# One down product of the last chunk as seven smaller products, with its token sums made earlier

## The chip, the cores and the metric

The kernel runs on one core of a Trainium2 chip. The metric is the device time of one execution in microseconds (us), as the median over runs. The core has TensorE (PE in the profile: matmuls; PEld: its weight loads), VectorE (DVE), ScalarE (ACT), GpSimd (POOL) and SyncE (SP, whose queue issues nearly all DMAs here). Matmuls write PSUM banks; the other data lies in SBUF.

## The reference

Four residual layers over x of 2048 tokens x 1024: linear attention, gated MLP, linear attention, gated MLP. The change touches the gated MLP:

```python
def _B_ref(x, W_gate, W_up, W_down):          # D = 1024, F = 3584
    gate = x @ W_gate                         # einsum bsd,df->bsf
    up = x @ W_up
    gate = gate * (gate > 0)
    h = gate * up
    return h @ W_down                         # einsum bsf,fd->bsd
x = x + _B_ref(_layernorm(x), W_gate, W_up, W_down)
```

## The kernel before, in words

Layers are numbered 0 to 3; the gated MLPs are 1 and 3. Each works on two chunks (c = 0, 1) of 1024 tokens, so (3, 1) is the very last chunk. A chunk has 14 gated units (u), each making two 128-wide pieces of h for all its tokens, and then the down stage (`down`).

All large products use the Strassen-Winograd scheme: a 2x2 block product by seven products, with sums of blocks before and after. In the gated units four banks of token sums (s1 to s4) and four sums of weights are used; the halves of tokens and of F give four blocks of h for each pair of units, kept in seven tiles hT[0..6]. In the down stage the seven products are called "11", "21", "T1", "T2", "22", "T3", "T4"; each is a 14-step accumulation over h, or over a sum of h blocks (e1, e2, third_sum), against a part of W_down or a sum of its parts. W_down's sums were made once, early, and lie in DRAM.

A down product is done in one of two ways:

- `product`: four banks of 128x512, 56 matmuls of 512 columns, weights in two ring entries of 896 KB, bank by bank handed to `done`.
- `deep`: the product is itself cut by the same scheme into seven products (1, 5, 6, 2, 7, 3, 4 in order of issue) of 14 matmuls of 256 columns on three banks x, y, z. Its token sums S1 to S4 are made on VectorE before (`inner`), its weight sums come from DRAM (`self.dd`, made by `make_dd`: load, four sums, seven stores), in four ring entries (`load_deep`; three of 896 KB, one of 448 KB). Between the products stand ScalarE copies (y from x after product 1, m5 from z after product 5) and one VectorE addition (z = y + m5 after product 6, line 1495). Products 7 and 4 accumulate on y, product 3 on z.

`is_deep` says which products of which chunk are deep. In (3, 1) the order is "11", "T2", "T1", "T3", "21", "22", "T4", and T1, 22, T4 and 21 are deep; "11" is a plain `product` on banks X. When a bank of "11" is done, `eleven_done` copies it to a bank of Y (ScalarE, line 1535), onto which T2 then accumulates, and adds it to the residual x (VectorE, line 1430).

The order of the work. TensorE, VectorE, ScalarE, GpSimd and SP each take their own instructions in the order in which the program was scheduled at build time. The scheduler walks the program in traced order: of the instructions of an engine that are ready by its own model, the one traced first goes first. The kernel places background work by ticks: `later.at(n, f)` traces f after n more ticks, one tick for each group of matmuls (four in a gated unit); `behind(self.last_put, ...)` keeps it on its engine behind the last `put` (the VectorE multiplication that writes h). A gated unit has 14 ticks, fewer where some of its products are made ahead (`inner_gi`): 10 in unit 12 of (3, 1), 12 in unit 13. Weights arrive through a ring of depth 5: reaching an entry traces the load of the one five places on. Ring entries, hT, e1, e2, s1 to s4, normalised tokens and `make_dd`'s two tiles share 16 buffers of 8 KB a partition, given out in traced order.

At the start of `down`, VectorE makes third_sum and, for each of seven tiles of h, e2 (line 1384) and e1 (line 1385); all are traced ahead of the first product. T2 uses e2, T1 uses e1.

In layer 1, chunk 1, the units also carry `ln_early` (layer norm statistics of the next layer), sums of the next layer's weights (`load_w`, `sums_w`), sums for later gated units (`make_gi`) and, from unit 6, `make_dd("T4")`. In (3, 1) the residual tiles x[0] to x[7], whose chunk is done, hold data of `inner_gi` (`ready_gi(5, 0, 2, 6)`, `ready_gi(6, ..., 4, 7)`) until unit 11.

Of the kernel before, what the change touches and what calls it, by code (L numbers as in the profile page):

```python
# [8 lines left out]
ALU = mybir.AluOpType  # L9
ACT = mybir.ActivationFunctionType  # L10
F32 = mybir.dt.float32
BF16 = mybir.dt.bfloat16
F16 = mybir.dt.float16
PSUM = bass.MemoryType.PSUM
P = 128
NW = 512
HD = 32
QT = 4
# [52 lines left out]
class _Later:  # L71
# [5 lines left out]
    def at(self, delay, fn):  # L77
        self.n += 1
        self.tasks.append((self.now + delay, self.n, fn))
# [13 lines left out]
class _Net:  # L93
# [903 lines left out]
                        out=t[:, 0:self.U // 2, :].bitcast(src.dtype), in_=src))  # L997

    T_AT = {"T1": 0, "T3": 1, "T4": 2, "T2": 3}
    DEEP = ("T1", "22", "T4", "21")  # L1000

    def is_deep(self, l, c, p):
        return p in {(1, 0): ("T1", "22"), (3, 1): self.DEEP}.get((l, c), self.DEEP[:3])

    def order_d(self, l, c):
        if (l, c) == (3, 1):
# [366 lines left out]
    def down(self, l, c, hT, final):  # L1373


        nc, later, ring, v = self.nc, self.later, self.ring, self.nc.vector
        N, H, NK = NW, NW // 2, self.U // 2
        pairs = [(p, [x[:, b::4, :] for b in range(4)]) for p, x in enumerate(hT)]
        e1, e2 = ([self.slot(f"e{i}_{l}_{c}_{k}", dtype=F16) for k in range(2)] for i in (1, 2))
        part = lambda e, p: e[p // 4][:, (p % 4) * 2:(p % 4) * 2 + 2, :]  # L1380
        with self.tc.issue_after(self.last_put.ins):
            self.third_sum(hT[-1])
            for p, (a, _, g, d) in pairs:
                v.tensor_tensor(out=part(e2, p), in0=d, in1=g, op=ALU.subtract)
                v.tensor_tensor(out=part(e1, p), in0=part(e2, p), in1=a, op=ALU.add)
        raw = lambda b: lambda k: hT[k // 2][:, (k % 2) * 4 + b, :]
        own = lambda e: lambda k: e[k // 8][:, k % 8, :]

        def of_h(b):
            return [([hT[p][:, b::4, :] for p in range(3)] + [hT[3][:, b:b + 1, :]]),  # L1390
                    ([hT[p][:, b::4, :] for p in range(4, 7)] + [hT[3][:, b + 4:b + 5, :]])]

        def of_e(e):
            return [[e[0][:, i:i + 2, :] for i in (0, 2, 4)] + [e[0][:, 6:7, :]],
                    [e[1][:, i:i + 2, :] for i in (0, 2, 4)] + [e[0][:, 7:8, :]]]

        def cut(pieces, j):
            return [x[:, :, j * H:(j + 1) * H] for x in pieces]

        def room(b):  # L1400
            return [cut(x, j) for x in of_h(b) for j in range(2)]

        X = [self.ps.tile([P, N], F32, tag="a", name=f"dx{j}") for j in range(QT)]
        Y = [self.ps3.tile([P, N], F32, tag="b", name=f"dy{j}") for j in range(2)]
        Y += [self.kvp.tile([P, N], F32, tag=f"kv{j}", name=f"dy{2 + j}") for j in range(2)]
        first, second = c * 2 * QT, (c * 2 + 1) * QT
# [30 lines left out]
                self.last_on = v.tensor_tensor(out=xo[:, s, :], in0=xs[:, s, :], in1=src[:, s, :], op=ALU.add)  # L1437
                queue.dma_start(out=self.o_v[:, ts.start + s.start:ts.start + s.stop, cols], in_=xo[:, s, :])

        def sums(ops):  # L1440

            for out, a, b, how in ops:
                for o, x, y in zip(out, a, b):
                    yield lambda o=o, x=x, y=y, how=how: v.tensor_tensor(out=o, in0=x, in1=y, op=how)

        def inner(A, S):
            S1, S2, S4, S3 = S
            (a11, a21), (a12, a22) = ([cut(A[k], j) for j in range(2)] for k in range(2))
            return (a11, a12, a22, S1, S2, S3, S4), list(sums((
                (S1, a21, a22, ALU.add), (S2, S1, a11, ALU.subtract),  # L1450
                (S3, a11, a21, ALU.subtract), (S4, a12, S2, ALU.subtract))))

        def deep(p, parts, put, cut_y=False):

            a11, a12, a22, S1, S2, S3, S4 = parts
            B = {}

            def entry(e):
                ring.free_before((l, c, p, e))
                w = self.deep_view(ring.get((l, c, p, e)))  # L1460
                raw = w if p[0] != "T" else w[:, :, :, :].bitcast(F16)
                made = w[:, :, :, :].bitcast(F16)
                B.update(({1: raw[:, 0], 5: made[:, 1]}, {6: made[:, 0], 2: raw[:, 1]},
                          {7: made[:, 0], 3: raw[:, 1]}, {4: made[:, 0]})[e])

            def mm(m, A, bank, start=False):
                for j in range(2):
                    out = bank[j] if isinstance(bank, list) else bank[:, j * H:(j + 1) * H]
                    for i in range(NK):
                        nc.tensor.matmul(out,  # L1470
                                         lhsT=A[i // 2][:, i % 2, j * P:(j + 1) * P], rhs=B[m][:, i, :],
                                         start=start and i == 0 and j == 0, stop=i == NK - 1,
                                         skip_group_check=True)
                    if m == 4 and cut_y:
                        put(1, 0, [out if i == j else None for i in range(2)], True)

            x, y, z = (self.ps.tile([P, N], F32, tag="a", name=f"d{n}{p}") for n in "xyz")
            m5 = self.temp(name="dm5")
            copy = lambda out, src: nc.scalar.activation(out=out, in_=src, func=ACT.Copy)
            halves = lambda a: [a[:, j * H:(j + 1) * H] for j in range(2)] if cut_y else [a]  # L1480
            ys = [y]
            if cut_y:
                ys = y = [y[:, 0:H], self.kvp.tile([P, N], F32, tag="kv0", name=f"dv{p}")[:, 0:H]]
            entry(0)
            mm(1, a11, x, True)
            for o, i in zip(ys, halves(x)):
                copy(o, i)
            later.tick()
            mm(5, S1, z, True)
            copy(m5, z)  # L1490
            later.tick()
            entry(1)
            mm(6, S2, y)
            for o, i, b in zip(halves(z), ys, halves(m5)):
                v.tensor_tensor(out=o, in0=i, in1=b, op=ALU.add)
            later.tick()
            mm(2, a12, x)
            put(0, 0, x, True)
            early = p != "T1"
            if early:  # L1500
                put(1, 1, m5, False)
            later.tick()
            entry(2)
            mm(7, S3, y)
            put(1, 1, y, early)
            later.tick()
            mm(3, S4, z)
            put(0, 1, z, True)
            if not early:
                put(1, 1, m5, True)  # L1510
            later.tick()
            entry(3)
            mm(4, a22, y)
            if not cut_y:
                put(1, 0, y, True)
            later.tick()

        def put_into(t, n):
            def put(j, h, src, last):
                if isinstance(src, list):  # L1520
                    for i, s in enumerate(src):
                        if s is not None:
                            at = t + 2 * j + i
                            onto(slice(at, at + 1), slice(n * N + h * H, n * N + (h + 1) * H), s, last,
                                 (nc.scalar, nc.sync)[i])
                    return
                onto(slice(t + 2 * j, t + 2 * j + 2), slice(n * N + h * H, n * N + (h + 1) * H), src, last)
            return put

        def put_both(j, h, src, last):  # L1530
            for a in range(2):
# [35 lines left out]
            to(first, 0, X, False)(j)  # L1567

        if self.is_deep(l, c, "21"):
            product("11", raw(0), X, True, eleven_done)  # L1570
            parts, jobs = inner(of_e(e1), room(0))
            spread(jobs, 1, 3)
            product("T2", own(e2), Y, False, to(first, 1, Y, False))
            for p, (_, b, _, _) in pairs:
                later.at(2 + p // 2, lambda b=b, p=p: sub(part(e2, p), b, part(e2, p)))
            deep("T1", parts, put_both)
            parts, jobs = inner(of_h(1), room(0))
            spread(jobs, 1, 3)
            product("T3", raw(2), Y, False, third_done)
            parts2, jobs = inner(of_e(e2), room(2))  # L1580
            spread(jobs, 1, 4)
            deep("21", parts, put_into(first, 0))
            parts, jobs = inner(of_h(3), room(0))
            spread(jobs, 1, 4)
            deep("22", parts2, put_into(first, 1))
            deep("T4", parts, put_into(second, 0), final and c == 1)
            return
# [20 lines left out]
    def plan_inner(self, l, c, u, hT):  # L1608
# [34 lines left out]
        if (l, c) == (3, 1):  # L1643
            if u == 0:
                at(4, lambda: ready(5, 0, 2, 6))
            if u == 1:
                at(4, lambda: ready(6, self.slot("gw", [P, 32 * P], F16), 4, 7))
        for m, us in self.INNER.get((l, c), {}).items():
            if u + 2 in us and (u + 2 - us[0]) % 2 == 0:
                at(10 if u + 2 == us[0] else 1, lambda m=m: self.load_gi(m, u + 2))  # L1650

    def layer_B(self, l, final):
# [6 lines left out]
        for c in range(2):  # L1659
# [3 lines left out]
            for u in range(self.U):  # L1663
# [26 lines left out]
                self.plan_inner(l, c, u, hT)  # L1690
                if u % 2 == 0 and u:
                    self.later.at(7, lambda h=hT[-2]: self.behind(self.last_put, self.third_sum, (h,)))
                if (l, c, u) in ((1, 1, 6), (3, 0, 5)):
                    self.make_dd("T4" if l == 1 else "21", 1)
                if c == 0 and u == 1:
                    for n, turn in enumerate(self.turns):
                        self.later.at(1 + n, turn)
# [75 lines left out]
```

## Time and profile before

| | |
|---|---|
| median of 3 runs | 1439.17 us (1439.04 to 1439.54) |
| span of the profiled execution | 1437.3 us |
| around the span, by the median | 1.9 us |
| PE busy | 1429.1 us (99%), 7706 matmuls |
| DVE busy | 1035.7 us (72%), 1991 instructions |
| ACT busy | 622.2 us (43%), 1137 instructions |
| "11" of the last chunk in the chain | 1354.23 us, for 12.09 us |
| mean DMA rate | 231 GB/s |

One execution was profiled; its own time is given by its span, with what lies around it taken from the median of the runs. Rows of a timeline give the start in us from the span's start, the duration, the engine, the source line, the operation, out<-in with the program's names and the number of instructions merged; in brackets, the idle time of the engine before it and what ended it. "SPq" rows are DMAs as SP's queue issues them. [...] A windows row gives the stretch, its length, and for PE, PEld, DVE, ACT and POOL the busy us and the number of instructions, then the granted TensorE clock, the DMA share and GB/s.

### The profile page before, as it was taken

How to read it: one execution, taken by the hardware profiler on the slowest of the kernel's cores; microseconds unless marked ns; L12 is line 12 of the kernel's file. 1: busy time of each engine (PE TensorE's matmuls, PEld its weight loads, DVE VectorE, ACT ScalarE, POOL GpSimd, SP SyncE). 2: the span in 40 equal slices, each digit the busy share in tenths (PEclk: the TensorE clock that was granted, in tenths of full speed). 3: DMA queues.
4: the chain of work that ended last, by engine and by line, in shares of the span. 5: the costliest groups of instructions: out<-in, count | busy, mean ns of one | idle time of the engine just before them, and what ended most of it. 6: DMA issues, size and time to landing. Idle time of an engine off the chain costs nothing.

```text
span 1437.3 us, 21281 instructions
## 1 busy us (share of the span) xinstructions
PE 1429.1 (99%) x7706; PEld 735.6 (51%) x7706; DVE 1035.7 (72%) x1991; ACT 622.2 (43%) x1137; POOL 309.0 (21%) x220
## 2 busy tenths in 40 slices
PE   9999999999999999999999999999999999999998
PEld 4444444444456444545654444445554565555457
DVE  7978698778685676558778885865766764666785
ACT  7873564233425234332058725733443434444201
POOL 1453860010100010110031577410111011111102
PEclk9999999999999999999999999999999999999999
DMA  9950787999659999866983118998878799775565
GB/s 284 243 162 8 171 208 201 292 317 292 204 190 308 350 355 334 278 216 209 292 281 100 60 22 248 278 281 261 263 226 297 225 305 281 215 203 170 175 238 180
DMA packets 360889, 331.31 MB, mean 231 GB/s; under 512 B 109840, under 2 KB 321296, under 8 KB 359760
## 3 DMA queue, kind: packets, MB, share of 16 engines
q1 hardware_dynamic: 352208, 307.15, 71.7%
q10 hardware_dynamic: 7136, 18.88, 3.5%
q0 software_dynamic: 1440, 3.93, 0.8%
q8 instruction: 60, 0.98, 0.3%
q14 instruction: 45, 0.37, 0.1%
HBM read 243.66 MB, written 61.60 MB: 212 GB/s over the span
## 4 chain that ended last, share of the span: by engine, by line
PE 94%; DVE 4%; ACT 1%; issue 0%; DMA 0%; DVEq 0%; ACTq 0%
PE ps L506 11%; PE yu L1275 9%; PE yg L1275 9%; PE dy L1417 8%; PE xg L1275 7%; PE xu L1275 6%; PE dx L1417 6%; PE i L1128 5%; PE ps L789 4%; PE zu L1275 3%; PE zg L1275 3%; PE my L588 3%; PE dyT L1470 2%; PE mv L588 2%; PE mx L588 2%; PE vu L1275 2%
## 5 line engine op out<-in xcount | busy, mean ns | idle before, releaser
L1275 PEld LDWEIGHTS <-w 128*128 128x128 f16 (+1 forms) x2768 | 270.6, 98 | 295.0 <-issue 3.7
L506 PE MATMUL ps<-w,xnT 128*128 128x512 bf16 x768 | 169.9, 379 | 0.7 <-DVE xnT L356 0.3
L1355 POOL TENSOR_TENSOR h<-m5u,m5g 128x512 f16<-128x512 f32 x28 | 37.1, 1326 | 423.4 <-DVE m5u L1351 253.4
L506 PEld LDWEIGHTS <-xnT 128*128 128x128 bf16 x768 | 74.3, 98 | 90.5 <-issue 1.8
L1275 PE MATMUL xg<-xnT,w 128*128 128x512 f16 x448 | 115.3, 379 | 0.0
L1275 PE MATMUL xu<-xnT,w 128*128 128x512 f16 x448 | 115.0, 379 | 0.0
L1417 PEld LDWEIGHTS <-h 128*128 128x128 f16 x672 | 65.7, 98 | 78.3
L1470 PEld LDWEIGHTS <-h 128*128 128x128 f16 x966 | 94.5, 98 | 12.3
L1355 POOL TENSOR_TENSOR h<-c22u,c22g 128x512 f16<-128x512 f32 x28 | 35.6, 1271 | 289.9 <-DVE c22u L1351 247.6
L1275 PE MATMUL yu<-s,w 128*128 128x512 f16 x376 | 96.5, 379 | 0.5 <-DVE zu L1331 0.5
L1275 PE MATMUL yg<-s,w 128*128 128x512 f16 x376 | 96.8, 379 | 0.0
L449 ACT ACTIVATE e<-e,eps 128x512 f32<-128x512 f32 x128 | 91.0, 720 | 3.2
L736 POOL TENSOR_TENSOR kvc<-pq,kvc 128x1024 f32<-128x1024 bf16 x32 | 78.6, 2455 | 53.1 <-DVE den L741 32.7
L1417 PE MATMUL dx<-w,h 128*128 128x512 bf16 x392 | 85.3, 379 | 0.0
L789 PE MATMUL ps<-T,pqT 128*128 128x512 bf16 x384 | 83.6, 379 | 0.0
L1302 DVE TENSOR_TENSOR h<-yu,r 128x512 f16<-128x512 f32 x56 | 38.6, 690 | 55.8 <-PE yu L1275 55.8
L1299 ACT ACTIVATE r<-yg 128x512 f32<-128x512 f32 x56 | 33.4, 597 | 101.5 <-PE yg L1275 101.5
L527 POOL TENSOR_TENSOR kvc<-kvc,slab 128x512 f32<-128x512 f32 x46 | 57.2, 1248 | 76.0 <-DVE slab L452 72.7
L448 ACT ACTIVATE e<-ps 128x512 f32<-128x512 f32 x92 | 54.2, 589 | 28.6 <-PE ps L506 28.1
L1128 PEld LDWEIGHTS <-x 128*128 128x128 f16 x504 | 49.2, 98 | 33.5 <-issue 1.9
L1299 ACT ACTIVATE r<-zg 128x512 f32<-128x512 f32 x56 | 32.8, 586 | 70.8 <-PE zg L1275 70.8
L748 POOL TENSOR_TENSOR pq<-pq,den 128x1024 bf16<-128x1024 bf16 x32 | 61.2, 1914 | 6.8 <-DVE den L743 6.8
(274 smaller groups left out, 2597.0 us busy)
## 6 DMA issues: line engine op xcount, KB each, us to landing
w<-in_B_W_gate_dram SPq DMA_DIRECT2D x56, 512.0 KB, 6.1
w<-in_B_W_up_dram SPq DMA_DIRECT2D x56, 512.0 KB, 5.4
w<-ddT SPq DMA_DIRECT2D x21, 896.0 KB, 6.3
w<-td SPq DMA_DIRECT2D x18, 896.0 KB, 4.8
x<-away SPq DMA_DIRECT2D x30, 512.0 KB, 7.5
w<-dd SPq DMA_DIRECT2D x15, 896.0 KB, 5.9
w<-in_B_W_down_dram SPq DMA_DIRECT2D x14, 896.0 KB, 6.1
away<-x SPq DMA_DIRECT2D x24, 512.0 KB, 6.8
```

Of the source, the lines that this page charges most:

```text
L449: self.last_exp = nc.scalar.activation(out=e, in_=e, func=ACT.Exp, scale=-1.0, bias=self.eps6[:, 0:1])
L506: nc.tensor.matmul(by_row(ps), lhsT=self.xnT[l, l_q][:, kt, j * P:(j + 1) * P], rhs=w[:, kt, :].rearrange("p (b i d) -> p i b d", i=R, d=H ...
L588: nc.tensor.matmul(banks[j], lhsT=A(i)[:, j * P:(j + 1) * P], rhs=B(i), start=start and i == 0, stop=i == NS - 1, skip_group_check=True)
L736: nc.gpsimd.tensor_tensor(out=prod, in0=pq_of[sc, j], in1=zrow, op=ALU.mult)
L748: nc.gpsimd.tensor_tensor(out=heads(pq), in0=heads(pq), in1=den[:, :].unsqueeze(2).to_broadcast([P, D // HD, HD]), op=ALU.mult)
L789: nc.tensor.matmul(ps, lhsT=pqT[sc][:, g, j * P:(j + 1) * P], rhs=T[g // 4][:, g % 4, n2 * NW:(n2 + 1) * NW], start=(g == 0), stop=(g == G ...
L1128: nc.tensor.matmul(b[:, w, :], lhsT=B[p][:, w, k, :], rhs=A[p][:, k, :], start=start and w == 0 and k == 0, stop=k == 1, skip_group_check= ...
L1275: nc.tensor.matmul(ps, lhsT=W[w][m][:, k, :], rhs=A[m][:, k, :], start=start and k == 0, stop=k == 3, skip_group_check=True)
L1299: self.last_relu = nc.scalar.activation(out=out, in_=ps, func=ACT.Relu)
L1355: nc.gpsimd.tensor_tensor(out=h[:, 3, :], in0=V["u"], in1=V["g"], op=ALU.mult)
L1417: nc.tensor.matmul(banks[j], lhsT=A(k)[:, j * P:(j + 1) * P], rhs=w[:, i, :], start=start and k == 0, stop=k == self.U - 1, skip_group_che ...
L1470: nc.tensor.matmul(out, lhsT=A[i // 2][:, i % 2, j * P:(j + 1) * P], rhs=B[m][:, i, :], start=start and i == 0 and j == 0, stop=i == NK - ...
```

## The change

"11" of (3, 1) becomes deep. `DEEP` gets "11" as a fifth member, so its weight sums are made in DRAM like those of the others: `make_dd("11", 1)` runs in layer 1, chunk 1, from unit 0 on. The ring of (3, 1) holds four entries for "11" in place of two.

The sixteen token sums of "11" (four kinds, four pieces each) are no longer work of the down stage: `first_sums` places twelve at ticks 1 to 6 of unit 12 and four, those that need h of units 12 and 13, at tick 7 of unit 13, into x[0], x[1], x[6] and x[7]. At the head of the down stage all e1 are traced behind all e2. The four banks X are not taken. `put_first` adds each finished block to the residual and copies it, in halves, to the banks of Y by ScalarE. Inside `deep`, for "11", the sum that ends in the second row's second block is first made in m5 (m5 = y + m5 after product 7) and put after product 3.

```diff
-    DEEP = ("T1", "22", "T4", "21")
+    DEEP = ("T1", "22", "T4", "21", "11")
...
+    def first_sums(self, hT, homes):
+        S = []
+        for t in homes:
+            h = self.x[t].bitcast(F16)[:, 0:self.U // 2 * (NW // 2)].rearrange("p (k n) -> p k n", n=NW // 2)
+            S.append([h[:, i:min(i + 2, 7), :] for i in range(0, 7, 2)])
+        self.first_parts, jobs = self.quarters(self.pieces(hT, 0), S)
+        return [jobs[i::4] for i in range(4)]
...
+            e1_of = lambda p, a: v.tensor_tensor(out=part(e1, p), in0=part(e2, p), in1=a, op=ALU.add)
             for p, (a, _, g, d) in pairs:
                 v.tensor_tensor(out=part(e2, p), in0=d, in1=g, op=ALU.subtract)
-                v.tensor_tensor(out=part(e1, p), in0=part(e2, p), in1=a, op=ALU.add)
+                if not self.is_deep(l, c, "11"):
+                    e1_of(p, a)
+            if self.is_deep(l, c, "11"):
+                for p, (a, _, _, _) in pairs:
+                    e1_of(p, a)
...
-            early = p != "T1"
+            early = p not in ("T1", "11")
...
             mm(7, S3, y)
-            put(1, 1, y, early)
+            if p == "11":
+                v.tensor_tensor(out=m5, in0=y, in1=m5, op=ALU.add)
+            else:
+                put(1, 1, y, early)
...
+        def put_first(j, h, src, last):
+            put_into(first, 0)(j, h, src, False)
+            for i in range(2):
+                nc.scalar.activation(out=Y[2 * j + i][:, h * H:(h + 1) * H], in_=src[:, i * H:(i + 1) * H],
+                                     func=ACT.Copy)
...
-            product("11", raw(0), X, True, eleven_done)
+            if self.is_deep(l, c, "11"):
+                deep("11", self.first_parts, put_first)
+            else:
+                product("11", raw(0), X, True, eleven_done)
...
+            if u == self.U - 2:
+                self.first = self.first_sums(hT, (0, 1, 6, 7))
+                for i, n in enumerate((3, 0, 1)):
+                    for k, job in enumerate(self.first[n]):
+                        at(1 + 2 * i + k // 2, lambda job=job: self.behind(self.last_put, lambda j: j(), (job,)))
+            if u == self.U - 1:
+                for job in self.first[2]:
+                    at(7, lambda job=job: self.behind(self.last_put, lambda j: j(), (job,)))
...
-                if (l, c, u) in ((1, 1, 6), (3, 0, 5)):
-                    self.make_dd("T4" if l == 1 else "21", 1)
+                if (l, c, u) in ((1, 1, 0), (1, 1, 6), (3, 0, 5)):
+                    self.make_dd({0: "11", 6: "T4", 5: "21"}[u], 1)
```

The functions `pieces`, `token_half` and `quarters` are the former inner functions `of_h`, `cut`, `sums` and `inner` of `down`, moved out so that `first_sums` can use them; for the other deep products they give the same instructions as before.

More of the change, by code (lines that the diff above doesn't have):

```diff
@@ L999, with pieces, token_half, quarters @@
     T_AT = {"T1": 0, "T3": 1, "T4": 2, "T2": 3}
-    DEEP = ("T1", "22", "T4", "21")
+    DEEP = ("T1", "22", "T4", "21", "11")
     def is_deep(self, l, c, p):
         return p in {(1, 0): ("T1", "22"), (3, 1): self.DEEP}.get((l, c), self.DEEP[:3])
+    def pieces(self, hT, b):
+        return [([hT[p][:, b::4, :] for p in range(3)] + [hT[3][:, b:b + 1, :]]),
+                ([hT[p][:, b::4, :] for p in range(4, 7)] + [hT[3][:, b + 4:b + 5, :]])]
+    def token_half(self, pieces, j):
+        return [x[:, :, j * NW // 2:(j + 1) * NW // 2] for x in pieces]
+    def quarters(self, A, S):
+        v = self.nc.vector
+        S1, S2, S4, S3 = S
+        (a11, a21), (a12, a22) = ([self.token_half(A[k], j) for j in range(2)] for k in range(2))
+        jobs = [lambda o=o, x=x, y=y, how=how: v.tensor_tensor(out=o, in0=x, in1=y, op=how)
+                for out, a, b, how in ((S1, a21, a22, ALU.add), (S2, S1, a11, ALU.subtract),
+                                       (S3, a11, a21, ALU.subtract), (S4, a12, S2, ALU.subtract))
+                for o, x, y in zip(out, a, b)]
+        return (a11, a12, a22, S1, S2, S3, S4), jobs
+    def first_sums(self, hT, homes):
[5 more added lines that the diff above has]
+        return [jobs[i::4] for i in range(4)]
     def order_d(self, l, c):
@@ L1382, in down @@
             self.third_sum(hT[-1])
+            e1_of = lambda p, a: v.tensor_tensor(out=part(e1, p), in0=part(e2, p), in1=a, op=ALU.add)
             for p, (a, _, g, d) in pairs:
                 v.tensor_tensor(out=part(e2, p), in0=d, in1=g, op=ALU.subtract)
-                v.tensor_tensor(out=part(e1, p), in0=part(e2, p), in1=a, op=ALU.add)
+                if not self.is_deep(l, c, "11"):
[3 more added lines that the diff above has]
+                    e1_of(p, a)
         raw = lambda b: lambda k: hT[k // 2][:, (k % 2) * 4 + b, :]
         own = lambda e: lambda k: e[k // 8][:, k % 8, :]
-        def of_h(b):
-            return [([hT[p][:, b::4, :] for p in range(3)] + [hT[3][:, b:b + 1, :]]),
-                    ([hT[p][:, b::4, :] for p in range(4, 7)] + [hT[3][:, b + 4:b + 5, :]])]
+        of_h = lambda b: self.pieces(hT, b)
         def of_e(e):
@@ L1395, in of_e @@
                     [e[1][:, i:i + 2, :] for i in (0, 2, 4)] + [e[0][:, 7:8, :]]]
-        def cut(pieces, j):
-            return [x[:, :, j * H:(j + 1) * H] for x in pieces]
         def room(b):
-            return [cut(x, j) for x in of_h(b) for j in range(2)]
-        X = [self.ps.tile([P, N], F32, tag="a", name=f"dx{j}") for j in range(QT)]
+            return [self.token_half(x, j) for x in of_h(b) for j in range(2)]
+        if not self.is_deep(l, c, "11"):
+            X = [self.ps.tile([P, N], F32, tag="a", name=f"dx{j}") for j in range(QT)]
         Y = [self.ps3.tile([P, N], F32, tag="b", name=f"dy{j}") for j in range(2)]
@@ L1438, in onto @@
                 queue.dma_start(out=self.o_v[:, ts.start + s.start:ts.start + s.stop, cols], in_=xo[:, s, :])
[L1440 to L1451, printed above, removed]
+        inner = self.quarters
         def deep(p, parts, put, cut_y=False):
```

## The prediction

> **What bounds the kernel now.** I read the page first (busy times, then the chain that ended last), then who TensorE (PE) waited for.
>
> ```profile
> span 1437.3 us, 21281 instructions
> PE 1429.1 (99%) x7706; PEld 735.6 (51%) x7706; DVE 1035.7 (72%) x1991; ACT 622.2 (43%) x1137; POOL 309.0 (21%) x220
> PE 94%; DVE 4%; ACT 1%; issue 0%; DMA 0%; DVEq 0%; ACTq 0%
> ```
>
> ```profile
> PE idle L302 <- DVE e L299: 1.4, 1, 1.4
> PE yu L1275 <- DVE zu L1331: 0.5, 1, 0.5
> ```
>
> TensorE is busy for 99% of the span and 94% of the chain; its longest single wait is 1.4 us, at the very start, and none of the others is above 0.5 us. So the time is the matmul stream. A change pays by what it takes from that stream, and loses by every hole it opens in it. Nothing else counts here. The span is 1437.3 us; the median of the runs is 1439.17 us, so 1.9 us lie around the span, and I carry those over unchanged. Then the chain at the place of the change, in order of time:
>
> ```profile
> 1354.23 12.09 PE dx L1417 x56
> 1366.31 12.09 PE dy L1417 x56
> 1378.40 1.53 PE dxT L1470 x14
> ...
> 1401.31 1.53 PE dx L1470 x14
> ```
>
> The columns are start, duration, group. The first row is the product "11" of the last chunk as it is; the second is T2; the last two are one of the seven small products of T1 (f16 weights) and of "21" (bf16 weights, as "11" has).
>
> **The change part by part.**
>
> **1. The matmuls.** 56 of 512 columns (12.09 us) go; 7 groups of 14 of 256 columns come, 7 x 1.53 = 10.71 us. The gain is 12.09 - 10.71 = 1.38 us, 0.10% of the time. It is the only term with a minus sign, and it is smaller than 0.2% (2.9 us), which is about what a measurement of this kernel can tell from no change.
>
> [...]
>
> **2. The sum that now stands between the products.** In the old "11" VectorE (DVE) fed nothing to TensorE until T1. In the new one the fifth product (S3, on the bank y) and the sixth (S4, on z) both need z = y + m5, a VectorE addition, done: the fifth overwrites what it reads, the sixth accumulates on what it writes. What VectorE does at that time:
>
> ```profile
> 1354.33 0.69 DVE L1302 TENSOR_TENSOR h<-yu,r 128x512 f16<-128x512 f32 x1 [1.04 <-PE yu L1275]
> 1354.94 0.68 DVE L1384 TENSOR_TENSOR e<-h 128x1024 f16<-128x1024 f16 x1
> 1355.54 0.68 DVE L1371 TENSOR_TENSOR h<-h 128x1024 f16<-128x1024 f16 x1
> ...
> 1361.56 1.28 DVE L1384 TENSOR_TENSOR e<-h 128x1024 f16<-128x1024 f16 x2
> 1362.77 1.28 DVE L1385 TENSOR_TENSOR e<-e,h 128x1024 f16<-128x1024 f16 x2
> 1363.97 1.27 DVE L1430 TENSOR_TENSOR x<-x,dx 128x512 f32<-128x512 f32 x2
> 1365.17 1.09 DVE L1444 TENSOR_TENSOR h<-e,e 128x512 f16<-128x512 f16 x3
> ...
> 1383.15 0.69 DVE L1495 TENSOR_TENSOR dzT<-dyT,dm 128x512 f32<-128x512 f32 x1
> ```
>
> ```profile
> 1361.88 0.58 ACT L1535 ACTIVATE dy<-dx 128x512 f32<-128x512 f32 x1 [7.82 <-PE dx L1417]
> ```
>
> ```profile
> 1354.06 6.21 PE L1417 MATMUL dx<-w,h 128*128 128x512 bf16 x28
> ```
>
> From 1354.94 to 1363.97 it makes the fifteen sums of the stage's head (third_sum, seven e2, seven e1) without a gap, 0.60 us apart. The change reorders the e1 behind the e2, but all fifteen stay ahead of the new product in the program. That program order decides is seen in the last rows: the first dx bank was ready for its addition once ScalarE's (ACT) copy of 1361.88 ended, at 1362.46, yet the addition ran at 1363.97, after two more e1. So z = y + m5 should run at 1363.97 and end 0.69 us later (the row of 1383.15 is the same operation in T1), at 1364.66. Without a wait the fifth product would start after four, at 1354.06 + 4 x 1.53 = 1360.18 (1354.06 is where the matmuls of "11" begin). The hole is 4.48 us. Nothing can fill it: the sixth product needs the same sum, the seventh comes after the fifth on y, T2 accumulates onto banks that the later products of "11" still have to seed, and T1 is behind weights whose buffers "11" still holds. Bounds: 0, if the sum is issued ahead of the e1; 5.1 us, if the fifteen start one operation later. I take 4.5, from the row itself.
>
> [...]
>
> **3. The rest of the product's tail.** Two ScalarE copies of 128x256 in place of one 128x512 for each block: 2 x 0.37 us (the row below), after an addition of 0.69 us, against a last product of 1.53 us; hidden, 0 (up to 0.3). VectorE's work in the old eleven_done (four additions) stays; z and the sum m5 are two more, 1.4 us, which later work makes up in idle stretches of T2 (the second row ends one of 0.69 us).
>
> ```profile
> 1424.33 0.37 ACT L1479 ACTIVATE dyT<-dxT 128x256 f32<-128x256 f32 x1 [8.57 <-PE dxT L1470]
> ```
>
> ```profile
> 1373.90 0.69 DVE L1430 TENSOR_TENSOR x<-x,dy 128x512 f32<-128x512 f32 x1 [0.69 <-PE dy L1417]
> ```
>
> **4. The weights on SyncE's (SP) queue.** Four ring entries (3 of 896 KB and one of 448) in place of two. The first three rows of loads for the old "11" and T2:
>
> ```profile
> 1343.87 0.34 SPq L996 DMA_DIRECT2D w<-td  x1
> 1354.26 0.34 SPq L996 DMA_DIRECT2D w<-td  x1
> 1354.69 0.38 SPq L1023 DMA_DIRECT2D w<-ddT  x1
> ```
>
> ```profile
> DMA to landing us min/median/max: 6.2/6.2/6.2
> ```
>
> These places in the queue (depth five) now carry entries 2 and 3 of "11" and the first of T2. The last one landed 6.2 us after its issue at 1354.69, at 1360.9; entry 2 is needed at 1360.2 but leaves at 1343.87, entry 3 leaves at 1354.26 for 1363.2, T2 needs its own at 1364.8. 0 us; a hole would have to come from a load 4 us later than these.
>
> **5. Sixteen token sums in units 12 and 13.** By the row of 1365.17 a 128x512 sum costs (1.09 - 0.42) / 2 = 0.33 us of VectorE, a 128x256 one 0.20 (rows below, 1366.77 to 1366.97); 12 x 0.33 + 4 x 0.20 = 4.8 us, 3.4 of them in unit 12.
>
> ```profile
> 1366.77 0.28 DVE L1444 TENSOR_TENSOR h<-e 128x256 f16<-128x256 f16 x1
> 1366.97 0.41 DVE L1444 TENSOR_TENSOR h<-h,e 128x512 f16<-128x512 f16 x1
> ```
>
> ```profile
> 1334.00:1344.00 10.00, 10.00 (x50) 4.69 (x48) 6.71 (x11) 3.41 (x7) 1.27 (x1) 1.00 0.27 92
> 1344.00:1354.00 10.00, 10.00 (x48) 4.49 (x46) 4.80 (x7) 3.42 (x6) 1.27 (x1) 1.00 0.52 185
> ```
>
> ```profile
> 1336.82 0.70 DVE L1331 TENSOR_TENSOR zg<-yg,x 128x512 f32<-128x512 f32 x1
> ```
>
> ```profile
> 1337.63 0.81 PE L1275 MATMUL yg<-s,w 128*128 128x512 f16 x3
> ```
>
> VectorE (fourth figure after the stretch: 6.71 and 4.80 us of 10) has 8.5 us free, so the work fits. But in unit 12 the sums are traced ahead of zg, and TensorE starts yg at 1337.63, 0.11 us after zg ends at 1337.52. Four sums (1.1 us) can come between; TensorE has the second product of u to do meanwhile. 0 to 1.5 us, taken 0.5, nearer the fit.
>
> **6. The weights' sums, made in layer 1, chunk 1.** make_dd("11") is 3 loads (1792 KB), 4 sums and 7 stores (3136 KB) in units 0 to 2.
>
> ```profile
> 490.00:500.00 10.00, 10.00 (x48) 4.45 (x46) 10.00 (x23) 4.29 (x10) 1.27 (x1) 1.00 1.11 337
> 500.00:510.00 10.00, 10.00 (x48) 4.55 (x47) 8.85 (x21) 4.58 (x8) 1.27 (x1) 1.00 1.06 358
> ```
>
> ```profile
> L1051 DVE TENSOR_TENSOR dd<-dd x4: 1079/1080/1083, 295.1 to 1042.4; 128x1792 f16<-128x1792 bf16 x4
> ```
>
> ```profile
> 498.80 0.67 DVE L1331 TENSOR_TENSOR zg<-yg,m5g 128x512 f32<-128x512 f32 x1
> ```
>
> ```profile
> 499.00 0.59 PE L1275 MATMUL vu<-s,w 128*128 128x512 f16 x2
> 499.52 1.02 PE L1275 MATMUL yg<-s,w 128*128 128x512 f16 x4
> ...
> 505.99 1.03 PE L1275 MATMUL xu<-xnT,w 128*128 128x512 f16 x4
> ```
>
> ```profile
> 485.64 1.96 SPq L1172 DMA_DIRECT2D w<-in_B_W_up_dram  x1
> ```
>
> Here VectorE is full (10.00 of 10, then 8.85) and the DMA engines too (shares 1.11 and 1.06), and TensorE starts yg at 499.52, 0.05 us after zg's end. Four sums of 1.08 us, 4.3 us, fall due from the middle of unit 1 on, ahead of such sums; TensorE has covered such lateness with the next unit's first products (vu at 499.00, two of its four matmuls, ahead of this unit's yg). 0 to 2.2 us (half of the 4.3), taken 0.5. The 4.9 MB at 350 GB/s are 14 us of transfers, in front of ring loads on SP's queue and, for the stores, held until VectorE's sums are done. The load issued at 485.64 feeds the matmuls of 505.99, 20 us later: 0, up to 1.
>
> **Sum.** -1.38 + 4.5 + 0.5 + 0.5 = +4.1 us: span 1441.4, time 1443.3 us, 0.29% slower.
>
> **The rivals.**
> *The wait is not there* (ends on the other side, not slower). The scheduler issues z = y + m5 between the e2 and the e1; eight sums end at 1354.94 + 8 x 0.60 = 1359.8, then z to 1360.5, a hole of 0.3 us. It decides at one point: whether z stands ahead of more than half of the e1. For it: the change does move the e1 back. Against: the held-back additions above. -1.38 + 0.3 + 0 to 1.0 = 1438.1 to 1439.1, no change that can be told.
> *The wait costs more than itself.* TensorE's first matmuls of the kernel, out of idleness, ran slow:
>
> ```profile
> 1.35 3.62 PE L302 MATMUL idle<-e 128*128 128x512 bf16 x10 [1.35 <-DVE e L299]
> ```
>
> Ten in 3.62 us, where ten at 216 ns and a drain of 0.16 take 2.3. If a hole of 4.5 us brings that back, 1.3 us come on top: 1444.6. Against it, no row shows a hole of that size. [...]
> *Parts 5 and 6 are the cost, not the wait.* Both at their ends: -1.4 + 0.3 + 1.5 + 2.2 = +2.6, 1441.8. Against it, TensorE showed no waits in those stretches.
>
> **How the numbers follow.** The forecast 0.55, no wait 0.27, wait and clock 0.13, the sums 0.05. Faster by over 0.2% would be below 1436.3; the only gain is 1.4 us, so 0.02. Within 0.2%: no wait, the sums, and the low end of the forecast (a hole of 3 us), 0.37. Slower 0.61. The range 1438.2 to 1446.0 runs from the rival without a wait to hole and clock with parts 5 and 6 high; the forecast's own is 1441.6 to 1445.2.
>
> **What would show it.** Part 1: groups of 14 at 1.53 us in the chain where the 56 were. Part 2: z's addition (written dz11) right behind the last e1, and a gap of some 4.5 us in TensorE before the fifth product, put down to VectorE. If z stands between e1 rows and the gap is under 1 us, the forecast falls. Parts 5 and 6: TensorE's waits for zg or zu near 1337 and near 500. Part 4: any TensorE wait for a DMA near 1360 would be a miss.

## The result and the profile after

The changed kernel takes 1459.8 us (median; 1458.59 to 1460.91). On the same chip the kernel before took 1439.36 us (1439.04 to 1440.42). The ratio is 1.0142, 95% interval 1.0128 to 1.0156: 1.4% slower. The prediction of 1443.3 us (1438.2 to 1446.0) had the sign and missed the size by 16.5 us. The profiled execution has a span of 1459.0 us, 21.7 above the span before; its own time, 1460.76 us, lies near the top of these runs. The account below is made against its span.

The page of the changed kernel, then TensorE's longest waits:

```profile
span 1459.0 us, 21395 instructions
...
PE 91%; DVE 4%; DMA 2%; ACT 1%; issue 1%; POOL 0%; SPq 0%; DVEq 0%; POOLq 0%; ACTq 0%
```

```profile
PE vu L1301 <- DMA w<-tu: 8.4, 1, 8.4
PE dy L1486 <- DVE dz L1511: 4.4, 1, 4.4
```

DMA was at 0% of the chain and is at 2%. The second row of the waits is the one that the prediction named. The first, twice as long, is a wait for a weight load, and it stands nowhere near the new product: it is in layer 1, chunk 1, where the weight sums of "11" are made. TensorE's timeline there (a row of several instructions lasts from the first start to the last end), and the same stretch in windows (columns as in the windows rows ahead; the last three figures are clock, DMA share and GB/s):

```profile
507.60 1.46 PE L1301 MATMUL vu<-s,w 128*128 128x512 f16 x3 [8.38 <-DMA w<-tu]
508.85 1.91 PE L1301 MATMUL yg<-s,w 128*128 128x512 f16 x4
```

```profile
500.00:510.00 10.00, 2.40 (x6) 0.87 (x7) 5.02 (x6) 0.00 (x0) 0.00 (x0) 0.61 1.01 310
510.00:520.00 10.00, 10.00 (x42) 4.29 (x41) 6.98 (x9) 4.40 (x8) 1.27 (x1) 0.88 1.08 363
```

After the hole four matmuls take 1.91 us instead of 1.03; the granted clock is 0.61 and 0.88 on average over the two windows. The deep "11" itself, in the chain of the changed kernel:

```profile
1376.00 3.70 DVE e L1409 x6
1379.69 0.62 DVE dz L1511
...
1380.36 3.14 PE dy L1486 x14
1383.50 2.95 PE dz L1486 x14
1386.45 1.53 PE dy L1486 x14
```

```profile
1376.04:1379.46 3.42, 0.00 (x0) 0.00 (x0) 3.42 (x7) 0.00 (x0) 0.00 (x0) 1.00 1.00 348
1379.46:1382.87 3.41, 2.51 (x12) 1.72 (x12) 3.41 (x10) 0.65 (x2) 0.00 (x0) 0.50 0.10 42
1382.87:1386.28 3.41, 3.41 (x17) 2.35 (x16) 2.64 (x7) 0.69 (x2) 0.00 (x0) 0.50 0.00 0
```

TensorE waits for six e1 and then for z (dz), 4.38 us, as forecast (4.48). Then two products take 3.14 and 2.95 us instead of 1.53, at a clock of 0.50. From the start of the first, 1380.36, to the start of T2 at 1387.82 the three products that end "11" take 7.46 us instead of 3 x 1.53 = 4.59, so 2.9 us more.

Comparing the start of the same matmul in both traces gives the account:

| where | us | prediction |
|---|---|---|
| layer 1, chunk 1, units 1 and 2: hole 8.4 and clock | +10.9 | part 6: 0.5 (0 to 2.2, and up to 1) |
| the same chunk, units 7 to 9 | +4.3 | none |
| units 12 and 13 of the last chunk | +0.3 | part 5: 0.5 |
| "11": fewer matmul columns | -1.4 | part 1: -1.4 |
| "11": hole before the fifth product (start to start) | +4.5 | part 2: 4.5 |
| "11": low clock after it | +2.9 | rival: 1.3 |
| small steps elsewhere | +0.1 | none |
| sum (before rounding) | +21.7 | +4.1 |

### The profile page after: what moved, and what is told of

It is laid out like the page before. It is cut to its first block, busy times and chain, and to the rows that moved or that the text cites. A ratio compares the mean times of both kernels' runs of the same rounds, so it can differ in the third digit from the quotient of the medians.

```text
span 1459.0 us, 21395 instructions
## 1 busy us (share of the span) xinstructions
PE 1435.5 (98%) x7748; PEld 742.1 (51%) x7748; DVE 1048.3 (72%) x2013; ACT 623.2 (43%) x1143; POOL 309.3 (21%) x220
## 4 chain that ended last, share of the span: by engine, by line
PE 91%; DVE 4%; DMA 2%; ACT 1%; issue 1%; POOL 0%; SPq 0%; DVEq 0%; POOLq 0%; ACTq 0%
PE ps L506 11%; PE yg L1301 8%; PE yu L1301 8%; PE dy L1444 7%; PE xu L1301 6%; PE xg L1301 6%; PE dx L1444 5%; PE i L1154 5%; PE ps L789 4%; PE zg L1301 3%; PE zu L1301 3%; PE my L588 3%; PE dy L1486 2%; PE dyT L1486 2%; PE mv L588 2%; PE mx L588 2%
## 5 line engine op out<-in xcount | busy, mean ns | idle before, releaser
L1444 PE MATMUL dx<-w,h 128*128 128x512 bf16 x336 | 73.0, 379 | 0.0
```

The costliest lines, as they stand in the source:

```text
L1444: nc.tensor.matmul(banks[j], lhsT=A(k)[:, j * P:(j + 1) * P], rhs=w[:, i, :], start=start and k == 0, stop=k == self.U - 1, skip_group_che ...
```

## The experiments

The theory after the result: two causes that do not need each other, W, the weight sums made in layer 1 (some 15 us), and Z, the z that VectorE makes late (some 6 us with its clock). Against W stood that the deep product itself, with its loads and sums, is the cost. Spans are compared with 1437.3 us (before) and 1459.0 us (changed). Where a kernel has one time only, effects of several us are read from it and its profile, no tenths of a per cent.

**The weight sums alone (`dd_alone`).** Before, plus the new `make_dd`, whose result nobody uses.

```diff
-                if (l, c, u) in ((1, 1, 6), (3, 0, 5)):
-                    self.make_dd("T4" if l == 1 else "21", 1)
+                if (l, c, u) in ((1, 1, 0), (1, 1, 6), (3, 0, 5)):
+                    self.make_dd({0: "11", 6: "T4", 5: "21"}[u], 1)
```

> The kernel before, with only the weight sums of "11" made in layer 1, chunk 1, and used by nobody. Theory W (the first hole and all that follows it in that chunk come from these loads, sums and stores): TensorE waits about 8 us near 499 us, and the time is about 15 us above before, 1454. Rival (the hole comes of something else that changed, for instance other places of the buffers): no hole, 1439 to 1441.

Measured: 1457.92 us, span 1456.2. TensorE waits 10.8 us for the same load. Ten DMAs and four sums alone bring 18.9 us of span, more than they do in the changed kernel, where the same load leaves 2.2 us earlier; the deep product is not needed for it.

**z ahead of the e1 (`z_first`).** The changed kernel, with the e1 traced behind z.

```diff
-                for p, (a, _, _, _) in pairs:
+                for p, (a, _, _, _) in pairs[:0]:
                     e1_of(p, a)
+        if self.is_deep(l, c, "11"):
+            for n, (p, (a, _, _, _)) in enumerate(pairs[0:]):
+                later.at(3 + n // 2, lambda p=p, a=a: e1_of(p, a))
```

> The changed kernel, with the seven e1 traced behind z = y + m5 (two to a tick) in place of ahead of it. Theory Z (the hole in "11" is the e1 ahead of that sum, and the slow clock after it is the hole's): hole of at most 0.3 us, matmuls behind it at full clock, some 6 to 7 us less than the changed kernel, about 1453. Rival (the hole is set by something else, such as the token sums or the fourth ring entry): still over 3 us, time within 2 us of the changed kernel.

Measured: 1456.19 us, span 1454.4. VectorE's and TensorE's timelines of this kernel:

```profile
1373.01 3.69 DVE L1411 TENSOR_TENSOR e<-h 128x1024 f16<-128x1024 f16 x6
1376.62 0.69 DVE L1514 TENSOR_TENSOR dz<-dy,dm 128x512 f32<-128x512 f32 x1
...
1377.84 2.49 DVE L1409 TENSOR_TENSOR e<-e,h 128x1024 f16<-128x1024 f16 x4
```

```profile
1377.36 1.69 PE L1489 MATMUL dy<-w,x 128*128 128x256 f16 x14 [0.16 <-DVE dz L1514]
...
1380.99 1.69 PE L1489 MATMUL dy<-w,h 128*128 128x256 f16 x14 [0.41 <-DVE dm L1525]
1383.25 12.25 PE L1447 MATMUL dy<-w,e 128*128 128x512 f16 x56 [0.57 <-ACT dy L1555]
```

With z right behind the e2 the 4.4 us are 0.16, and two small waits appear later (0.41, 0.57). No product is slow any more. From the start of "11" to the end the kernel now loses 0.2 us, where the changed kernel loses 6.0, so Z is worth 5.8 us, just under the 6 to 7 expected. The time fell by less, 3.6 us and not to 1453, because the hole in layer 1 stays, as it must if it has another cause, and is longer in this kernel (9.6 us against 8.4).

**The weight sums elsewhere (`dd_moved`, `both`).** The changed kernel with `make_dd("11")` in layer 3, chunk 0, unit 3, its sums 8 + 2n steps after the loads (18 + 4n before), first alone, then with z first.

```diff
-                if (l, c, u) in ((1, 1, 0), (1, 1, 6), (3, 0, 5)):
-                    self.make_dd({0: "11", 6: "T4", 5: "21"}[u], 1)
+                if (l, c, u) in ((1, 1, 6), (3, 0, 3), (3, 0, 5)):
+                    self.make_dd({3: "11", 6: "T4", 5: "21"}[u], 1)
```

> The changed kernel, with the weight sums of "11" made in layer 3, chunk 0, from unit 3 on (sums 8 ticks after the loads and 2 apart, to be through before those of "21"), where the DMA share was about 0.8. Theory W: no hole near 499, about 15 us less than the changed kernel, 1444 to 1445. Rival (4.9 MB and four sums cost as much wherever they are put): 1455 or more, with a hole near 990.

> Both edits at once. Theories W and Z together: what is left is -1.4 us from the matmuls, +0.5 from the sums in units 12 and 13 and up to 0.3 of the hole: 1438.3 to 1439.0, within 0.2% of before. If one of them is wrong: 1444 or more.

Measured: 1451.26 us (span 1449.4) alone. With z first 1445.37 us (1444.41 to 1447.79), ratio to before 1.0048, interval 1.0035 to 1.0062. Layer 1 loses nothing in both, but the new place has a late load of its own; the waits of the first and of the second kernel:

```profile
PE dy L1486 <- DVE dz L1511: 4.4, 1, 4.4
PE i L1154 <- DMA x<-gi: 4.3, 1, 4.3
```

```profile
PE i L1154 <- DMA x<-gi: 2.3, 1, 2.3
```

So both expectations missed, 1444 to 1445 for the move alone and no difference from before for the two together: near 1035 us the first kernel loses 7.0 us, the second 3.9. Taking the work away from one place was right; the other place was not prepared for it. What makes a place bad needed its own runs.

**Order on the queue, or bytes (`dd_later_stores`, `dd_loads`, `dd_no_sums`, `dd_no_stores`)?** `dd_alone` with the three stores of raw blocks 14 steps after the loads, not 4.

```diff
-        self.later.at(4, lambda: self.store_dd(p, ((0, b11), (3, b21), (5, b22))))
+        self.later.at(4 if p != "11" else 14, lambda: self.store_dd(p, ((0, b11), (3, b21), (5, b22))))
```

> Kernel before plus the weights' sums of "11" in layer 1, chunk 1 (made and stored, used by nobody), with one shift: the three raw-block stores are put on SyncE's queue 14 steps after their loads instead of 4, so that they no longer wait there for blocks that are still landing. Theory Q (order on the queue: the ring load of the next up weight stood behind stores that waited): that load leaves near 486 again and TensorE's hole near 499 goes from 10.8 us to under 2; span 1438 to 1446. Theory B (bytes: 4.9 MB into DMA engines that are already at a share of 1.1): the order doesn't matter, holes of the same sum stay, wherever they land; span 1453 to 1458.

And with the loads alone: no store and no sum.

```diff
-        self.later.at(4, lambda: self.store_dd(p, ((0, b11), (3, b21), (5, b22))))
+        if p != "11":
+            self.later.at(4, lambda: self.store_dd(p, ((0, b11), (3, b21), (5, b22))))
...
-        for n in range(4):
+        for n in range(4 if p != "11" else 0):
```

> Kernel before plus the three loads of the raw blocks of "11" (1792 KB) in layer 1, chunk 1; left out are all seven stores and the four VectorE sums. If the loads alone stand in the way (B: bytes, 1792 KB at 350 GB/s = 5.1 us of full DMA engines in front of the ring load): a hole of 3 to 6 us near 499, span 1441 to 1446. If the waiting stores or the sums made the hole (Q, or VectorE): no hole over 1 us, span 1437.5 to 1439.

Two more were made of `dd_alone`: one without the four sums, one without the seven stores.

```diff
-        self.nc.vector.tensor_tensor(out=out, in0=a, in1=b, op=ALU.subtract)
+        if p != "11":
+            self.nc.vector.tensor_tensor(out=out, in0=a, in1=b, op=ALU.subtract)
```

> dd_alone without the four VectorE sums of "11" (left out: the sums; the three loads and all seven stores stay, at the same steps, so 4.9 MB move). If the bytes and the order on the queue are the cost: within 2 us of dd_alone's span of 1456.2 us, with a hole of 8 to 11 us at 499. If VectorE is a good part of it (its sums hold the stores back, and the units' own sums): under 1450.

```diff
-        for m, b in blocks:
+        for m, b in blocks if p != "11" else ():
```

> dd_alone without the seven stores of "11" (left out: the stores; loads and sums stay, 1.8 MB move). If VectorE's 4.3 us cost nothing beside the loads: the span of dd_loads, 1440.3 (1439.5 to 1441.5). If the four sums cost what the prediction allowed at most, 2.2 us: 1442.5; more than 1443 would say that the sums are a cause of their own.

Measured: later stores 1455.95 us (span 1454.2), loads only 1442.11 (1440.3), no sums 1452.84 (1451.1), no stores 1448.82 (1447.0). None of the theories holds as it was stated. With the stores later the hole at 499 fell from 10.8 to 4.1 us, not under 2; other holes grew, and the span fell by 2.0 us only. The loads alone cost 3.0 us, with a hole of 2.15. Without the sums the span fell by 5.1 us, between the two bounds set, and the hole was 3.2 us, not 8 to 11. The kernel without stores was far above the 1443 that had been set as the sign that the sums are a cause of their own. Above the span before, then: loads 3.0 us, loads and sums 9.7, loads and stores 13.8, all of them 18.9. Sums and stores both count. The rows say part of why. First SyncE's queue in the loads-only kernel, then in `dd_alone`, with its waits:

```profile
484.93 6.62 SPq L1034 DMA_DIRECT2D dd<-in_B_W_down_dram  x3
491.65 0.73 SPq L1173 DMA_DIRECT2D w<-in_B_W_up_dram  x1
492.44 2.87 SPq L1177 DMA_DIRECT2D w<-tu  x1
```

```profile
488.29 7.04 SPq L1034 DMA_DIRECT2D dd<-in_B_W_down_dram  x3
499.32 0.37 SPq L1042 DMA_DIRECT2D dd<-dd  x1
499.79 0.50 SPq L1172 DMA_DIRECT2D w<-in_B_W_up_dram  x1
501.83 0.97 SPq L1042 DMA_DIRECT2D dd<-dd  x2
502.86 2.17 SPq L1176 DMA_DIRECT2D w<-tu  x1
```

```profile
SPq L1042 <- DMA dd<-in_B_W_down_dram: 5.4, 2, 3.9
```

The load that TensorE waits for is w<-tu (the sums of W_up for unit 2). Before, it stood on the queue two us behind the load of 485.64:

```profile
487.65 2.86 SPq L1176 DMA_DIRECT2D w<-tu  x1
```

```profile
w<-tu SPq DMA_DIRECT2D x1, 512.0 KB, 9.0
```

It landed at 487.65 + 9.0 = 496.7, and vu, which it feeds, started at 499.00: 2.3 us of room. In every other kernel here the load lands later (the starts of vu are from the timelines of TensorE; rows for loads only and `dd_alone`):

```profile
501.31 1.04 PE L1276 MATMUL vu<-s,w 128*128 128x512 f16 x4 [2.15 <-DMA w<-tu]
```

```profile
510.35 1.46 PE L1275 MATMUL vu<-s,w 128*128 128x512 f16 x3 [10.78 <-DMA w<-tu]
```

| kernel | w<-tu issued | landed | vu starts | hole |
|---|---|---|---|---|
| before | 487.65 | 496.67 | 499.00 | none |
| loads only | 492.44 | 501.26 | 501.31 | 2.15 |
| later stores | 494.45 | 503.26 | 503.31 | 4.13 |
| loads and sums, no stores | 495.05 | 503.86 | 503.91 | 4.63 |
| changed | 500.62 | 507.55 | 507.60 | 8.38 |
| loads and stores, no sums | 502.39 | 509.94 | 509.99 | 3.19 |
| `dd_alone` | 502.86 | 510.30 | 510.35 | 10.78 |

In every kernel of the table but the first, vu starts 0.05 us after the load lands, whatever else differs. How long TensorE idles for it depends on a second thing: what stands ahead of vu in its program order. Without the sums the load lands nearly as late as with them, yet the hole is 3.19 us:

```profile
500.60 1.02 PE L1276 MATMUL yg<-s,w 128*128 128x512 f16 x4 [1.36 <-DVE zg L1332]
...
509.99 1.89 PE L1276 MATMUL vu<-s,w 128*128 128x512 f16 x4 [3.19 <-DMA w<-tu]
```

From the first of these rows on TensorE does seven groups, 6 us, that the scheduler has put ahead of vu. In the other changed kernels of the table vu stands ahead of yg, and TensorE did nothing while it waited, 2.15 to 10.78 us. In the loads-only kernel zg ended at 500.46, but yg, which needs it, started at 502.18, behind vu. And yg itself would have been late in `dd_alone`. It needs zg, which VectorE makes behind the first of the four sums, and that sum waits for a DMA:

```profile
503.09 1.09 DVE L1051 TENSOR_TENSOR dd<-dd 128x1792 f16<-128x1792 bf16 x1 [2.81 <-DMA dd<-dd]
504.10 0.69 DVE L1331 TENSOR_TENSOR zg<-yg,m5g 128x512 f32<-128x512 f32 x1
```

zg ends at 504.79 there, in the kernel without sums at 500.54. Why the scheduler chose another order of vu no run shows.

Now the issue of w<-tu. From 487.65 to 492.44, 4.8 us, is the three loads standing ahead on the queue. Two to 2.6 us more come in the kernels that use the loaded tiles (494.45 and 495.05): there the loads themselves leave later, behind waits for a buffer (1.8 and 1.4 us) and for earlier work. Of the remaining 8.4 us, 494.45 to 502.86, the loads' later start is 1.35 (488.29 against 486.94). The rest is the stores of raw blocks, which stand on the queue ahead of w<-tu and wait for their loads to land (5.4 us of waits). The DMA engines of `dd_alone` were idle for little of this wait: their share was 1.10 up to 499 and 0.51 and 0.73 in the two us after it. So the order on the queue is the larger part of this load's delay and the three loads are the smaller. It is not the larger part of the time: with the three stores moved, the waits for x<-gi grew from 2.4 to 4.5 us, and 2.0 us of span were won. In the kernel without stores the excess over loads only is the 2.5 us of longer hole, slow matmuls behind it (the hole of 2.15 us was followed by none) and 1.2 us of waiting for zg.

While the stores of raw blocks waited, nothing else left SyncE's queue: in the rows of `dd_alone` no DMA is issued from 495.33, where the loads' row ends, to 499.32, nor from 500.29 to 501.83, and w<-tu left behind the last of them, at 502.86.

Units 7 to 9 lose 4 to 9 us more in every kernel that has the seven stores (5.3 in `dd_alone`) and 0.6 or 1.6 in the two without them. In the changed kernel the load x<-gi of unit 8 leaves at 578.67, before at 558.99, and ahead of it stands again a store that waits for a load, here of T4's weight sums:

```profile
SPq L1068 <- DMA ddT<-td: 6.0, 1, 6.0
```

That this wait alone is the cause there is not shown. In the loads-only kernel such stores wait too (5.7 us, with x<-gi behind them), and little is lost; T4's loads leave there at 551.24, in the changed kernel at 566.82. No run took the wait away, and what delays T4's loads stays open.

**How long a hole before the clock falls (`z_mid`)?** The changed kernel with four e1 ahead of z and three behind (the diff of "z ahead of the e1" with `pairs[:4]` and `pairs[4:]`).

> The changed kernel with four of the seven e1 traced ahead of z = y + m5 and three behind it. By the program order on VectorE z ends 3 x 0.60 = 1.8 us earlier, and the hole in "11" is 4.38 - 1.8 = 2.6 us. Theory S (the clock falls only after a hole of some length between 2.6 and 4.4 us): no granted clock under 0.95 after it, and the start of T1 lies 4.6 to 5.0 us earlier against the kernel's own earlier offset than in the changed kernel (1.8 of hole and about 3 of clock). Theory L (every hole costs some clock, in proportion): about 1.8 us lost at a lower clock after it, 3.0 us earlier in all.

Measured: 1457.85 us, span 1456.1. The wait, and the clock behind it:

```profile
PE dy L1489 <- DVE dz L1514: 2.6, 1, 2.6
```

```profile
1376.25:1379.66 3.41, 0.99 (x10) 0.88 (x10) 3.38 (x8) 0.36 (x2) 0.00 (x0) 1.00 0.75 242
1379.66:1383.08 3.42, 3.42 (x19) 2.44 (x17) 2.48 (x5) 0.97 (x4) 0.00 (x0) 0.50 0.07 29
```

The hole is the 2.6 us that program order gives. The clock falls to 0.50 all the same, a microsecond after the matmuls have started again, so theory S, a threshold between 2.6 and 4.4 us, is out. The last three products of "11" take 6.25 us (1378.67 to 1384.92) instead of 4.58, 1.7 us more, as theory L had it for this hole; the longer holes do not keep its proportion (last section).

**A place with room (`dd_at31`).** z first with the e1 behind both additions onto m5, ScalarE's two copies in `put_first` traced ahead of its addition, and `make_dd("11")` in unit 2 of the last chunk, its stores further behind (14 steps after the loads, 4 after each sum). The excerpt below does not show the edits of the stores and of `put_first`.

```diff
-                if (l, c, u) in ((1, 1, 0), (1, 1, 6), (3, 0, 5)):
-                    self.make_dd({0: "11", 6: "T4", 5: "21"}[u], 1)
+                if (l, c, u) in ((1, 1, 6), (3, 0, 5), (3, 1, 2)):
+                    self.make_dd("11" if c and l == 3 else {6: "T4", 5: "21"}[u], 1)
...
+                later.at(5 + n // 2, lambda p=p, a=a: e1_of(p, a))
```

> The changed kernel with e1 behind both additions onto m5 (z first), the two copies to the second banks traced ahead of the first block's addition, and the weights' sums of "11" made in units 2 to 4 of the last chunk itself, where the DMA engines' share is 0.36 to 0.9 and VectorE is busy for 4 to 7 of 10 us; raw stores 14 steps after the loads, those of the sums 4. If the place in the program was the cost: no hole over 0.6 us anywhere, -1.38 + 0.5 + 0.3 = -0.6 us, 1438.4 (1437.6 to 1439.4), at best the same as before. If the 4.9 MB and four sums cost wherever they stand: again 3 us or more of holes in units 2 to 5, 1442 to 1448.

Measured: 1439.04 us (1438.23 to 1439.73) against 1439.55 (1438.93 to 1441.31): ratio 0.9994, interval 0.9985 to 1.0003. No difference from before that can be measured, and 1.4% better than the change as made. Its longest wait after the kernel's first, the product of "11" behind the former hole, and the stretch in which the sums are made, here and in the kernel before:

```profile
PE dy L1447 <- DMA w<-td: 0.7, 1, 0.7
```

```profile
1362.14 1.69 PE L1489 MATMUL dy<-w,x 128*128 128x256 f16 x14 [0.16 <-DVE dz L1514]
```

```profile
1210.00:1220.00 10.00, 10.00 (x55) 5.28 (x54) 4.67 (x7) 4.21 (x9) 1.27 (x1) 1.00 1.10 326
1220.00:1230.00 10.00, 10.00 (x60) 5.72 (x59) 6.02 (x9) 4.29 (x8) 1.27 (x1) 1.00 1.01 291
```

```profile
1210.00:1220.00 10.00, 10.00 (x58) 5.39 (x56) 4.35 (x7) 4.67 (x9) 1.27 (x1) 1.00 0.50 150
1220.00:1230.00 10.00, 10.00 (x60) 5.72 (x59) 6.27 (x10) 4.34 (x8) 1.27 (x1) 1.00 0.84 239
```

With the work in it the DMA engines are as full here (1.10, 1.01) as in layer 1, and TensorE does not wait at all, so a full share alone does not make a hole. But this place had room in two ways: the share before was 0.50 and 0.84, in layer 1 1.11 and 1.06, and the stores come later. Which of these made it good, and how much room its loads have, was not separated. This kernel contains all of the change's work, so that work as such can be had for less than this comparison can tell. The gain of part 1 is too small to be told from the times; in the trace it is there: from the start of "11" to the start of T2 are 11.02 us (1355.70 to 1366.72) where there were 12.09.

## Why the prediction was wrong

- **Part 6 failed**, and it is 14.7 of the 17.6 us by which the account exceeds the sum: 15.2 us measured in layer 1, chunk 1, against 0.5. Three errors stand in it. The prediction took the queue's row of 485.64 and the matmuls that need it 20 us later. The matmuls at 499.00, quoted in the same part, use the load issued next on that queue, at 487.65; its room was 2.3 us. It counted the seven stores as bytes "held until VectorE's sums are done", but did not ask what is queued behind a store that waits; three of the seven wait for no sum, they wait for the loads just in front of them, at a place where a load of 512 KB took 9.0 us to land. And it named vu as what TensorE does while zg is late, with VectorE's cost bounded by 2.2 us; vu is the very product whose load came late, and leaving out the four sums alone was worth 5.1 us of span. The 10.9 us at the first hole are the late load and the slow matmuls behind it; for the 4.3 us of units 7 to 9 the cause stays open.
- **Part 2 was right**: hole 4.38 us against 4.48, in program order, and the order of the e1 alone removes it (0.16 us in `z_first`).
- **The clock rival (the wait costs more than itself) was right in kind and mis-sized**: 1.3 us from the first matmuls of the kernel, 2.9 us measured, at a granted clock of 0.50. Its chance of 0.13 was the author's estimate, which the kernel before, with no wait over 1.4 us, could not show; it was left out of the sum. With the hole right, the clock had to be in the forecast.
- **Parts 1, 3 and 4** hold: groups of 14 at 1.53 us (109 ns for a matmul of 256 columns, against 12.09 us / 56 = 216 ns for one of 512), T2 behind the last product without a wait, no wait for a weight load near 1376. Part 3's zero had cover, though: once the hole was gone in the kernel with z first, the tail showed 0.41 and 0.57 us, above the 0.3 allowed.
- **Part 5** holds in size, 0.3 us in units 12 and 13 against 0.5; TensorE's wait there was for another VectorE addition (yg, 0.24 us) than the zg that was named. Of the 4.8 us of sums, 3.6 fall into unit 12, not 3.4, which changes nothing.
- **The rival of parts 5 and 6** named the right place with a ceiling of 2.2 us, so its time of 1441.8 was as far off as the forecast.

## What to carry to other kernels

Before work is put into "idle" time far from the edit, find on each queue it uses the load with the least room (when it lands against when its matmuls start), ask what the new DMAs do to that one, and look at what stands behind its matmuls in TensorE's program order. A busy share under 1 is no proof of room: in layer 3 it was about 0.8, and 3.9 to 7.0 us were lost. In `dd_alone` stores that waited 5.4 us for their data held the loads issued behind them on that queue, so a store belongs late enough that its data has landed. And a TensorE hole is to be priced with the slow matmuls after it: one of 2.33 us was followed by a clock of 0.50 here, and after one of 2.6 us that cost 1.7 us more.

## What was not expected of the hardware

The granted clock fell after a hole as short as 2.33 us, and where a hole lay counted beside its length. In the changed kernel the clock is either 1.00 or 0.50, and its changes at 502.23, 512.47, 1379.46 and 1386.28 lie 10.24, 866.99 and 6.82 us apart, 3, 254 and 2 times 3.413 us; figures between, such as 0.61, are averages over a window. Cut into stretches of that length, the kernel with both edits, then loads only, then later stores read:

```profile
1031.24:1034.66 3.42, 1.39 (x7) 0.43 (x5) 3.42 (x6) 0.30 (x1) 0.00 (x0) 1.00 1.07 350
1034.66:1038.07 3.41, 3.10 (x11) 1.63 (x12) 1.20 (x3) 0.86 (x2) 0.00 (x0) 0.50 1.15 304
```

```profile
497.04:500.45 3.41, 2.11 (x10) 0.68 (x7) 3.41 (x8) 0.18 (x1) 0.00 (x0) 1.00 1.11 337
500.45:503.86 3.41, 2.55 (x12) 1.19 (x13) 2.94 (x5) 0.00 (x0) 0.00 (x0) 1.00 1.10 335
```

```profile
579.72:583.13 3.41, 1.58 (x7) 0.48 (x5) 0.51 (x1) 0.63 (x1) 0.00 (x0) 1.00 0.94 285
583.13:586.54 3.41, 1.34 (x9) 0.89 (x10) 0.64 (x2) 1.76 (x4) 0.00 (x0) 1.00 1.11 322
```

A stretch with TensorE busy for 1.39 or 1.34 us was followed by the low clock, one with 1.58 was not; so in these runs 2.02 and 2.07 us of idleness within one stretch were followed by the fall and 1.83 were not (busy times rest on modelled ends). The hole of 2.33 us put 2.02 into one stretch and was followed by 0.50; the one of 2.15 us was cut into 1.30 and 0.86, and the clock stayed at 1.00. The low clock lasted one to three stretches: it ended after one with 3.10 us busy, not after one with 2.51. Its cost is about half of the time that matmuls run in it: in "11" a product took 3.14 us at 0.50 instead of 1.53. After holes of 2.6, 4.4, 4.6 and 8.4 us it was 1.7, 2.9, 2.8 (16 matmuls from 503.91 to 510.17, 6.26 us instead of 3.46, without stores) and 2.2 us (20 from 507.60 to 514.10, 6.50 instead of 4.32, changed kernel): not in proportion to the hole. The same hole of 4.4 us in "11" cost 1.7 us in `dd_moved`, where one stretch was slow instead of two.
